# Exponents formed on ScalarE in five narrowings, and another opening of batch 0, in a Fourier-mixing and gated-convolution kernel

## The chip, the cores and the metric

The kernel runs on one core of one Trainium2 chip. The metric is device time in microseconds: the median of several executions. A profile is one further execution, recorded by the hardware profiler; its times count from the start of its span.

## The reference

```python
def _attn_ref(x):                       # x: (8, 3136, 256) float32
    X = np.fft.fft(x, axis=1)
    X = np.fft.fft(X, axis=2)
    return X.real.astype(np.float32)

def _moe_ref(x, w_in, conv_w, w_out):   # w_in 256x1024, conv_w 3x1024, w_out 1024x256
    h = np.maximum(x @ w_in, 0.0)
    # conv_out[s] = sum over k of conv_w[k] * h[s + k - 1], zeros outside
    gate = 1.0 / (1.0 + np.exp(-conv_out))
    return (h * gate @ w_out).astype(np.float32)

def reference(x, moe_w_in, moe_conv_w, moe_w_out):
    return _moe_ref(_attn_ref(x), moe_w_in, moe_conv_w, moe_w_out)
```

The three weights arrive as float64 (the division by a numpy float64 root makes them so); `x` and the output are float32.

## The kernel before

**The mathematics as the kernel lays it out.** The real part of a two-dimensional Fourier transform is computed by products with cosine and sine tables. Symmetry halves both axes: rows of `x` are folded with their mirrored rows (`fold_ops`, lines 143 to 200, on VectorE, with small parts on GpSimd), and the feature axis likewise. The sequence transform gives two spectra of a batch, `pt` and `qt` (`PQ[b]`), with 1569 columns. The feature transform is not done on its own: it is multiplied into `w_in` once, into the tile `G`, by `blocks(i)` for four blocks of `w_in`.

A hidden row `h` is then relu(a + c) in front and relu(a - c) behind, where a comes from `pt` and c from `qt`. Feature D/2 of the spectrum doesn't fit into the 128 rows of a product. It is kept as one row, `er[0]` for batch 0, spread to 128 partitions (`eb`), and added by ScalarE: `seed` writes `eb` times a weight column (`ge`, made by `column(i)`) into the PSUM tile `pa` before the product accumulates onto it.

**Turns.** The main loop runs over steps (batch, chunk, filter): 8 batches, 4 chunks of columns, 8 filters of 128 hidden features; 32 steps a batch. The order on each engine is the order of emission (`manual_schedule`): turn t emits, in this order, the sigmoid of step t-2, the products and copies of step t+1, side work "act", `combine` of step t, side work "dve", `seed` of step t+2, the first tap of step t, the other two taps of step t-1, the gate of step t-2, side work "load", the output products of step t-3, and side work "pe". Side work is put into turns by `at(turn, place, fn)`.

- `products` (L653 before): `pb` from `qt` and `pa` from `pt`, on TensorE. In a "triple" step (batch 0, the first 20 steps) a third product adds c to `pa` too, so that ScalarE can write the front half of `h` by a Relu straight from `pa` (`copies`, L672). In the other steps ScalarE copies `pb` twice (L675) and VectorE forms both halves (`combine`, L686).
- The taps: the first on ScalarE (L692), the other two on VectorE (L698, two instructions of 770 elements). The gate: half on GpSimd (L718), half on VectorE (L719).
- `mm2`: six or seven products with `w_out` into `po` (L733), and in the last filter the copies out and the stores on SP.

PSUM: `psa` has two tiles (`pa`), `psb` one (`pb`), `psd` one (`pd`), `pso` four (`po`, shared with the opening's `spare()`).

**Narrowing float64 weights.** `narrow` (L508) makes a float32 from the two 32-bit words of a float64 in seven VectorE operations: exponent bits out (L515), rebias (L516), shift back (L517), sign in (L518), mantissa top with hidden bit (L520), add the low word (L521), multiply (L522). It runs in four pieces for `w_in` (128x512 each), once for the convolution weights, and in four pieces for `w_out`, in turns 2, 3, 5 and 7; the last piece of `w_in` is in turn 0.

**The opening of batch 0.** TensorE is kept busy by products whose result is not used (`keep_on`), then the units of the sequence transform run: four odd ones, then by hand the units 2, 4, 3, 7, 8, where 2, 3, 7 and 8 are the even ones and 4 is the feature unit. Each unit has matmuls, a ScalarE copy and a `fin`: VectorE operations (L291 and L294 for even units), or four GpSimd operations for the feature unit (L353, L354), which complete `er[0]`. `row()` brings `er[0]`'s first content by a DMA; `flip()` (L366) negates every fourth column on ScalarE; `store()` writes the row to DRAM (`ed`); `spread` (L463) reads it back to all partitions, one transfer a chunk, into the four buffers of `eb`.

In batch 0's first four steps (`FIRST`) no `eb` is used: a product with one contraction row, `left[0:1]` by `er[0]`, adds feature D/2 to `pa` on TensorE; its weights are made in `blocks(0)` and `blocks(1)`. The `pa` tiles of steps 4 and 5 are first written over all 512 columns by a product (`start_all`, L640)[...]. The feature rows of batches 1 to 7 come from class `Feature`, whose tile takes the place of `er[0]` in its pool of one buffer.

Of the kernel before, what the change touches and what calls it, by code (L numbers as in the profile page):

```python
# [26 lines left out]

TRIPLE = 20  # L30
FIRST = 4
RC = 56
NQ = 8
CUTS = (0, 384, 768, 1152)
# [4 lines left out]
def kernel(  # L39
# [23 lines left out]
    NF = F // P  # L63
# [6 lines left out]
    const = ctx.enter_context(tc.tile_pool(name="const", bufs=1))  # L70
# [4 lines left out]
    ebp = ctx.enter_context(tc.tile_pool(name="ebp", bufs=4))  # L75
# [14 lines left out]
    stt = nc.vector.scalar_tensor_tensor  # L90
    act = nc.scalar.activation

    def mm(o, l, r, start, stop):
        nc.tensor.matmul(o, l, r, start=start, stop=stop, skip_group_check=True)  # L94

    def spare():

        return pso.tile([P, 2, D], F32, name="po", tag="po").rearrange("p a d -> p (a d)")
# [4 lines left out]
    xh, wt, ea = {}, {}, {}  # L103
# [3 lines left out]
    sg = const.tile([P, 2, 2], F32, name="sg")  # L107
# [97 lines left out]
    PQ, eb, er = {}, {}, {}  # L205
# [257 lines left out]
    def spread(b, cs):  # L463

        for c in cs:
            ch = chunks[c]
            eb[b, c] = ebp.tile([P, HN], F32, name="eb", tag="eb")[:, 0:ch.k1 - ch.k0]
            nc.sync.dma_start(out=eb[b, c], in_=ed[b:b + 1, ch.k0:ch.k1].to_broadcast([P, ch.k1 - ch.k0]))
# [36 lines left out]

    def narrow(dst, raw):  # L508

        ts = nc.vector.tensor_scalar  # L510
        lsl, lsr = ALU.logical_shift_left, ALU.logical_shift_right
        lo, hi = raw[:, :, :, 0], raw[:, :, :, 1]
        lof, d = lo.bitcast(F32), dst.bitcast(I32)

        ts(out=d, in0=hi, scalar1=20, scalar2=0x7FF, op0=lsr, op1=ALU.bitwise_and)  # L515
        ts(out=d, in0=d, scalar1=-896, scalar2=0, op0=ALU.add, op1=ALU.max)  # L516
        ts(out=d, in0=d, scalar1=23, scalar2=None, op0=lsl)  # L517
        stt(out=d, in0=hi, scalar=-0x80000000, in1=d, op0=ALU.bitwise_and, op1=ALU.bitwise_or)  # L518

        ts(out=hi, in0=hi, scalar1=0xFFFFF, scalar2=0x100000, op0=ALU.bitwise_and, op1=ALU.bitwise_or)  # L520
        stt(out=lof, in0=lo.bitcast(U32), scalar=2.0 ** -32, in1=hi, op0=ALU.mult, op1=ALU.add)  # L521
        stt(out=dst, in0=lof, scalar=2.0 ** -20, in1=dst, op0=ALU.mult, op1=ALU.mult)  # L522

    class Weight:

# [7 lines left out]
        def load(self, eng):  # L533
            if self.raw is None:
                eng.dma_start(out=self.dst, in_=self.src)
            else:
                eng.dma_start(out=self.raw.rearrange("p c n e -> p c (n e)"), in_=self.src)

        def narrow(self, c0, c1):
            if self.raw is not None:  # L540
                narrow(self.dst[:, c0:c1], self.raw[:, c0:c1])

    ident = gp.tile([3 * NF, 3 * NF], F32, name="ident", tag="g")
    make_identity(nc, ident)
    cw24 = gp.tile([3 * NF, 1, P], F32, name="cw24", tag="g")
# [10 lines left out]
    dm = gp.tile([P, 2, 2, P], F32, name="dm", tag="g")  # L556
    N4 = F // 4
# [28 lines left out]

    def blocks(i):


        w = w4[i]  # L590
        for g in range(2):
            p = spare()
            for t in range(2):
                mm(p[:, 0:N4], dm[:, t, g, :], w[:, t], t == 0, t == 1)
            nc.scalar.copy(out=G[:, g, i * N4:(i + 1) * N4], in_=p[:, 0:N4])
        if 2 * i < FIRST:
            p = spare()
            for t in range(2):
                mm(p[0:1, N4:2 * N4], dm[:, t, 1, P - 1:P], w[:, t], t == 0, t == 1)
            nc.scalar.copy(out=left[0:1, 2 * i:2 * i + 2].rearrange("p f i -> p (f i)"), in_=p[0:1, N4:2 * N4])  # L600
        if i > 1:
            column(i)

    def column(i):
        w, p = w4[i], spare()
        for m in range(NF // 4):
            for t in range(2):
                mm(p[:, m:m + 1], w[:, t, m * P:(m + 1) * P], dm[:, t, 1, P - 1:P], t == 0, t == 1)
        nc.scalar.copy(out=ge[:, i * NF // 4:(i + 1) * NF // 4], in_=p[:, 0:NF // 4])
# [7 lines left out]
    rows = out.rearrange("b s d -> (b s) d")  # L617
    hs, gs, pa, pb, po, nb = {}, {}, {}, {}, {}, {}

    def start_all(p, l, r):  # L620

        mm(p, l, r, True, True)

    def cut(s):
        b, c, f = s
        ch = chunks[c]
        return ch, ch.k1 - ch.k0, slice(f * P, (f + 1) * P)

    def first(s):

        return s[0:2] == (0, 0) and s[2] < FIRST

    def seed(s):

        b, c, f = s
        ch, n, fs = cut(s)
        pa[s] = psa.tile([P, 512], F32, name="pa", tag="pa")
        if not first(s):
            if s in ((0, 0, FIRST), (0, 0, FIRST + 1)):
                start_all(pa[s].rearrange("p (t n) -> p t n", t=2), dm[:, 0, 0], w4[0])  # L640
            act(pa[s][:, 0:n], eb[b, c], AF.Copy, scale=ge[:, f:f + 1])  # L641

    def triple(s):

        return s[0] == 0 and s[1] * NF + s[2] < TRIPLE

    def row_of(s):
        hs[s] = hp.tile([P, HW], F32, name="h", tag="h")
# [4 lines left out]
    def products(s):  # L653
        b, c, f = s
        ch, n, fs = cut(s)
        pb[s] = psb.tile([P, 512], F32, name="pb", tag="pb")
        mm(pb[s][:, 0:n], G[0:P - 1, 1, fs], PQ[b][1][0:P - 1, ch.k0:ch.k1], True, True)
        mm(pa[s][:, 0:n], G[:, 0, fs], PQ[b][0][:, ch.k0:ch.k1], first(s), not triple(s))
        if first(s):
            mm(pa[s][:, 0:n], left[0:1, f, :], er[b][:, ch.k0:ch.k1], False, False)  # L660
        if triple(s):
            mm(pa[s][:, 0:n], G[0:P - 1, 1, fs], PQ[b][1][0:P - 1, ch.k0:ch.k1], False, True)

    def copies(s):

        ch, n, fs = cut(s)
        p = pb.pop(s)
        nb[s] = nbp.tile([P, 2, HN], F32, name="nb", tag="nb")
        if triple(s):
            act(nb[s][:, 1, ch.cols], p[:, ch.cols], AF.Copy, scale=-2.0)  # L670
            row_of(s)
            act(hs[s][:, ch.front], pa[s][:, ch.fcols], AF.Relu)  # L672
# [34 lines left out]
    def sigmoid(s):  # L707

        v, p, r = shares(s)
        for c in (slice(p.start, r.stop), v):  # L710
            act(gs[s][:, c], gs[s][:, c], AF.Sigmoid)  # L711
# [33 lines left out]
    taps()  # L745
    idle = psb.tile([P, 512], F32, name="pb", tag="pb")

    def keep_on(n):

        for _ in range(n):  # L750
            mm(idle[:, 0:2 * P], wt[0][1][0:NP, 1, 0], wt[0][1][0:NP, 0, 0:2], True, True)

    begin, us, row, flip, store = units(0)
    begin()
# [4 lines left out]

    odds = [us[j] for j in (0, 1, 5, 6)]  # L760
    w_in[0].narrow(0, 2)
    keep_on(16)
    mirror_tables(0)
    mend_row(1, half)
    mirror_tables(2)
# [10 lines left out]
                    w_out.load(nc.sync)  # L776
    mend_row(0, half)
    w_in[1].narrow(0, 2)
    for i, u in enumerate(us[j] for j in (2, 4, 3, 7, 8)):
        u.matmuls(0, 1)  # L780
        u.copy()
        u.fin()
    flip()
    store()
    spread(0, range(len(chunks)))
    for f in load_ops(1, 0, nc.sync):
        f()
    blocks(0)
# [5 lines left out]
    def at(cycle, where, fn):  # L794
        side.setdefault((cycle, where), []).append(fn)

    for i in (1, 2, 3):
        at(i - 1, "pe", lambda i=i: blocks(i))
    at(0, "dve", lambda: w_in[3].narrow(0, 2))
    for i in (0, 1):  # L800
        at(i, "pe", lambda i=i: column(i))
    for cycle, c in ((2, 0), (3, 2), (5, 4), (7, 6)):
        at(cycle, "dve", lambda c=c: w_out.narrow(c, c + 2))
    for j, fn in enumerate(load_ops(1, 1, nc.sync)):
        at(NF + 1 + j // 3, "load", fn)

# [57 lines left out]
    seed(steps[1])  # L864
    products(steps[0])
    copies(steps[0])
    for t in range(n + LAG):
        def run(where):
            for fn in side.get((t, where), []):
                fn()  # L870
        if 0 <= t - 2 < n:
            sigmoid(steps[t - 2])
        if t + 1 < n:
            products(steps[t + 1])
            copies(steps[t + 1])
# [12 lines left out]
        run("load")  # L888
        if t >= LAG:
            mm2(steps[t - LAG])  # L890
        run("pe")
# [66 lines left out]
```

## Time and profile before

| what | value |
|---|---|
| median of 10 runs | 1218.14 us (1217.46 to 1219.17) |
| profiled execution, its own time | 1219.29 us |
| its span | 1217.5 us |
| TensorE busy | 1185.7 us, 97% of the span |
| VectorE busy | 1124.8 us, 92% |
| ScalarE busy | 877.8 us, 72% |
| GpSimd busy | 373.4 us, 31% |
| chain that ended last, by engine | PE 69%, DVE 21%, issue 4%, ACT 2%, DMA 1% |

The profiled execution took 1.79 us more than its span, and 1.15 us more than the median. PE is TensorE, PEld its weight loads, DVE VectorE, ACT ScalarE, POOL GpSimd, SP the engine that issues most DMAs. A busy share is a mean over stages with different limits, so the stages are to be read one by one. Most of the work is recorded under one line for TensorE (L94, the helper `mm`), so its rows are told apart by tiles.

### The profile page before, as it was taken

What the parts mean: (1) busy time and instruction counts of PE and PEld (TensorE: products, weight loads), DVE (VectorE), ACT (ScalarE), POOL (GpSimd) and SP (SyncE); (2) the same over time, 40 slices, a digit from 0 to 9 for tenths busy, and PEclk for the clock granted to TensorE, in tenths of its full rate; (3) what the DMA queues carried; (4) which work ended last, traced back from release to release, by engine and by line L of the source; (5) the groups of instructions that cost most, each with busy time, mean ns of one, the idle gap of its engine ahead of it and who ended that gap; (6) DMA issues with size and microseconds to landing.
All of it is one profiled execution on the core that took longest, in us unless ns stands there. A gap on an engine that the chain in (4) does not pass through costs nothing.

```text
span 1217.5 us, 15448 instructions
## 1 busy us (share of the span) xinstructions
PE 1185.7 (97%) x4876; PEld 906.8 (74%) x4876; DVE 1124.8 (92%) x1696; ACT 877.8 (72%) x1832; POOL 373.4 (31%) x474
## 2 busy tenths in 40 slices
PE   5999999999999999999999999999999999999998
PEld 4676777677777777777777777777777777777776
DVE  7799999999999999998999999999998988899996
ACT  2466656676777777777777777777777777788884
POOL 5224524343334232424224242332222222222222
PEclk9999999999999999999999999999999999999999
DMA  9622243211121110302122020210001000110000
GB/s 218 198 8 80 80 49 100 68 53 41 40 87 50 60 46 1 107 26 73 34 73 61 5 80 27 88 46 26 27 1 53 31 26 27 46 33 27 26 27 31
DMA packets 70213, 66.30 MB, mean 54 GB/s; under 512 B 28123, under 2 KB 57827, under 8 KB 70131
## 3 DMA queue, kind: packets, MB, share of 16 engines
q1 hardware_dynamic: 64493, 52.18, 15.2%
q0 software_dynamic: 5120, 12.85, 3.5%
q8 instruction: 39, 0.64, 0.2%
q14 instruction: 43, 0.35, 0.1%
q10 hardware_dynamic: 518, 0.28, 0.1%
HBM read 39.53 MB, written 25.74 MB: 54 GB/s over the span
## 4 chain that ended last, share of the span: by engine, by line
PE 69%; DVE 21%; issue 4%; ACT 2%; DMA 1%; DVEq 0%; SPq 0%; ACTq 0%
PE po L94 43%; PE pb L94 10%; PE pa L94 10%; DVE g L698 7%; PE pd L94 6%; DVE h L686 3%; DVE g L719 3%; DVE xh L158 2%; ACT nb L675 1%; DVE xh L169 1%; DVE w L186 1%; DVE w L187 1%; DMA xh<-in_x_dram 0%; DVE xh L173 0%; DVE pt L291 0%
## 5 line engine op out<-in xcount | busy, mean ns | idle before, releaser
L94 PE MATMUL po<-wout,g 128*128 128x256 f32 x3072 | 709.0, 380 | 10.9 <-DVE g L719 10.3
L94 PEld LDWEIGHTS po<-wout,g 128*128 128x128 f32 x3072 | 578.7, 190 | 164.0 <-DVE g L719 43.6
L698 DVE SCALAR_TENSOR_TENSOR g<-h,cw,g 128x770 f32<-128x770 f32 (+1 forms) x512 | 548.7, 1072 | 9.3 <-ACT g L692 0.2
L718 POOL TENSOR_TENSOR g<-g,h 128x385 f32<-128x385 f32 (+1 forms) x256 | 234.1, 915 | 767.0 <-ACT g L711 496.1
L711 ACT ACTIVATE g<-g 128x385 f32<-128x385 f32 (+2 forms) x512 | 244.1, 526 | 191.4 <-DVE g L698 188.9
L675 ACT ACTIVATE nb<-pb 128x386 f32<-128x386 f32 (+2 forms) x472 | 208.0, 493 | 85.6 <-PE pb L94 84.6
L686 DVE CUSTOM_DVE_ANT_0 h<-pa,nb 128x386 f32<-128x386 f32 (+2 forms) x492 | 255.5, 559 | 3.7 <-ACT h L672 3.7
L692 ACT ACTIVATE g<-h,cw 128x770 f32<-128x770 f32 (+1 forms) x256 | 243.2, 950 | 0.2 <-DVE h L686 0.2
L94 PE MATMUL pb<-qt,G 127*128 127x387 f32 (+2 forms) x512 | 212.6, 496 | 0.0
L94 PE MATMUL pa<-pt,G 128*128 128x387 f32 (+2 forms) x512 | 211.8, 494 | 0.0
L641 ACT ACTIVATE pa<-eb,ge 128x387 f32<-128x387 f32 (+2 forms) x252 | 151.4, 601 | 1.3 <-PE pa L94 0.7
L94 PEld LDWEIGHTS pa<-pt,G 128*128 128x128 f32 x512 | 96.8, 189 | 73.6 <-issue 18.2
L719 DVE TENSOR_TENSOR g<-g,h 128x385 f32<-128x385 f32 (+1 forms) x256 | 146.1, 571 | 0.9 <-ACT g L711 0.9
L94 PE MATMUL pd<-tab,w 98*128 98x196 f32 (+3 forms) x448 | 126.7, 374 | 0.0
L133 POOL DMA_INDIRECT xh<-in_x_dram,idx x64 | 105.5, 1649 | 13.3 <-issue 9.2
L94 PEld LDWEIGHTS pb<-qt,G 127*128 127x128 f32 x512 | 94.0, 190 | 17.9 <-issue 1.4
L94 PEld LDWEIGHTS pd<-tab,w 98*128 98x128 f32 (+1 forms) x448 | 84.7, 191 | 12.3
L738 ACT COPY os<-po 128x256 f32<-128x256 f32 x196 | 57.4, 393 | 8.2 <-PE po L94 4.6
L158 DVE TENSOR_TENSOR xh<-xh 98x1020 f32<-98x1020 f32 (+1 forms) x32 | 40.7, 1277 | 3.4 <-DMA xh<-in_x_dram,idx 3.4
L169 DVE TENSOR_TENSOR xh<-xh 98x1024 f32<-98x1024 f32 (+1 forms) x32 | 41.3, 1290 | 0.1
L188 POOL COPY w<-xh 98x4 f32<-98x4 f32 (+1 forms) x32 | 20.2, 632 | 28.0 <-DVE xh L169 14.8
L291 DVE TENSOR_TENSOR qt<-as,pd 128x197 f32<-128x197 f32 (+1 forms) x14 | 7.2, 514 | 20.3 <-ACT as L287 20.3
(114 smaller groups left out, 394.0 us busy)
## 6 DMA issues: line engine op xcount, KB each, us to landing
out_dram<-os SPq DMA_DIRECT2D x192, 128.0 KB
xh<-in_x_dram SPq DMA_DIRECT2D x16, 784.0 KB
eb<-ed SPq DMA_DIRECT2D x16, 193.5 KB
tab<-dft_seq_dram SPq DMA_DIRECT2D x4, 589.5 KB
raw<-in_moe_w_in_dram SPq DMA_DIRECT2D x4, 512.0 KB
raw<-in_moe_w_out_dram SPq DMA_DIRECT2D x1, 2048.0 KB
eb<-ed SPq DMA_DIRECT2D x8, 209.0 KB
eb<-ed SPq DMA_DIRECT2D x8, 193.0 KB
```

Source lines behind the costliest of these rows:

```text
L94: nc.tensor.matmul(o, l, r, start=start, stop=stop, skip_group_check=True)
L133: nc.gpsimd.indirect_dma_start(out=xh[b, h][0:NP, 7 - m].rearrange("p q d -> p (q d)"), out_offset=None, in_=bass.AP(tensor=x.tensor, offs ...
L158: vt(a[:, :, :, 1:D], a[:, :, :, 1:D], r[:, :, :, D - 1:0:-1], op=ALU.add)
L641: act(pa[s][:, 0:n], eb[b, c], AF.Copy, scale=ge[:, f:f + 1])
L675: act(nb[s][:, i, cols], p[:, cols], AF.Copy, scale=-1.0 if i else 1.0)
L686: nc.vector._custom_dve(TENSOR_ADD_SAT, out=to, in0=a[:, cols], in1=c[:, i, cols], s0=BIG, s1=0.0)
L692: act(gs[s], hs[s][:, 0:n], AF.Copy, scale=cw[:, 0, s[2]:s[2] + 1])
L698: stt(out=g, in0=h[:, k:k + n], scalar=cw[:, k, f:f + 1], in1=g, op0=ALU.mult, op1=ALU.add)
L711: act(gs[s][:, c], gs[s][:, c], AF.Sigmoid)
L718: gt(g[:, p], g[:, p], h[:, p], op=ALU.mult)
L719: vt(g[:, v], g[:, v], h[:, v], op=ALU.mult)
L738: nc.scalar.copy(out=osb[:, j % 2], in_=pt[:, j % 2])
```

## The change

Seven edits, in three groups.

1. `narrow` can be given a scratch tile (`room`, the upper half of `left`). Then rebias and shift are one ScalarE activation, a Relu with scale 2^23 and a bias tile `low` of -896 x 2^23; the sign comes in after the mantissa, and the masked mantissa goes to `room`. It is split: `power` (one VectorE operation and the Relu) is emitted in a new place "first", after the sigmoid; `product` (four VectorE operations) stays in "dve". This form is used in five narrowings: the last of `w_in`, and all four of `w_out`. The other three of `w_in` keep seven operations.
2. Triple steps begin at step 3 instead of 0. Steps 0 to 2 copy `pb` twice and form both halves on VectorE.
3. `FIRST` and what belongs to it goes: the one-row products in steps 0 to 3, their weights in `blocks`, and `start_all`. All steps are seeded. The feature unit becomes the first of the five units, followed by `flip`, `store` and the spread of chunks 1 to 3; chunk 0's `eb` comes from a product of a row of ones with `er[0]` on TensorE and a ScalarE copy. `column(0)` and `column(1)` move ahead. The keep-on products become 8 of 512 columns instead of 16 of 256, two of them into the `pa` tiles. There are two more small memsets at the start.

```diff
-TRIPLE = 20
-FIRST = 4
+TRIPLE = 3, 20
...
+    low = const.tile([P, 1], F32, name="low")
+    nc.gpsimd.memset(low, -896.0 * 2 ** 23)
+    def narrow(dst, raw, room=None):
...
+        sg = hi
+        if room is not None:
+            c, n = hi.shape[1:]
+            sg = room[:, 0:c * n].rearrange("p (c n) -> p c n", c=c)
+        def power():
+            ts(out=d, in0=hi, scalar1=20, scalar2=0x7FF, op0=lsr, op1=ALU.bitwise_and)
+            if room is not None:
+                act(d, d, AF.Relu, scale=2.0 ** 23, bias=low[0:d.shape[0]])
+            else:
+                ts(out=d, in0=d, scalar1=-896, scalar2=0, op0=ALU.add, op1=ALU.max)
+                ts(out=d, in0=d, scalar1=23, scalar2=None, op0=lsl)
+        def sign():
+            stt(out=d, in0=hi, scalar=-0x80000000, in1=d, op0=ALU.bitwise_and, op1=ALU.bitwise_or)
+        def product():
+            if room is None:
+                sign()
+            ts(out=sg, in0=hi, scalar1=0xFFFFF, scalar2=0x100000, op0=ALU.bitwise_and, op1=ALU.bitwise_or)
+            stt(out=lof, in0=lo.bitcast(U32), scalar=2.0 ** -32, in1=sg, op0=ALU.mult, op1=ALU.add)
+            if room is not None:
+                sign()
+            stt(out=dst, in0=lof, scalar=2.0 ** -20, in1=dst, op0=ALU.mult, op1=ALU.mult)
+        return power, product
...
+    one = const.tile([1, P], F32, name="one")
+    nc.gpsimd.memset(one, 1.0)
...
-        if 2 * i < FIRST:
-            p = spare()
-            for t in range(2):
-                mm(p[0:1, N4:2 * N4], dm[:, t, 1, P - 1:P], w[:, t], t == 0, t == 1)
-            nc.scalar.copy(out=left[0:1, 2 * i:2 * i + 2].rearrange("p f i -> p (f i)"), in_=p[0:1, N4:2 * N4])
...
-        if not first(s):
-            if s in ((0, 0, FIRST), (0, 0, FIRST + 1)):
-                start_all(pa[s].rearrange("p (t n) -> p t n", t=2), dm[:, 0, 0], w4[0])
-            act(pa[s][:, 0:n], eb[b, c], AF.Copy, scale=ge[:, f:f + 1])
+        act(pa[s][:, 0:n], eb[b, c], AF.Copy, scale=ge[:, f:f + 1])
...
-        return s[0] == 0 and s[1] * NF + s[2] < TRIPLE
+        return s[0] == 0 and TRIPLE[0] <= s[1] * NF + s[2] < TRIPLE[1]
...
-        mm(pa[s][:, 0:n], G[:, 0, fs], PQ[b][0][:, ch.k0:ch.k1], first(s), not triple(s))
-        if first(s):
-            mm(pa[s][:, 0:n], left[0:1, f, :], er[b][:, ch.k0:ch.k1], False, False)
+        mm(pa[s][:, 0:n], G[:, 0, fs], PQ[b][0][:, ch.k0:ch.k1], False, not triple(s))
...
-    keep_on(16)
+    keep_on([idle] * 6)
+    keep_on([psa.tile([P, 512], F32, name="pa", tag="pa") for _ in range(2)])
...
-    for i, u in enumerate(us[j] for j in (2, 4, 3, 7, 8)):
+    for i, u in enumerate(us[j] for j in (4, 2, 3, 7, 8)):
         u.matmuls(0, 1)
         u.copy()
         u.fin()
-    flip()
-    store()
-    spread(0, range(len(chunks)))
+        if i == 0:
+            flip()
+            store()
+            spread(0, range(1, len(chunks)))
+    n = chunks[0].k1
+    p = psd.tile([P, 512], F32, name="pd", tag="pd")
+    mm(p[:, 0:n], one, er[0][:, 0:n], True, True)
+    eb[0, 0] = ebp.tile([P, HN], F32, name="eb", tag="eb")[:, 0:n]
+    nc.scalar.copy(out=eb[0, 0], in_=p[:, 0:n])
+    column(0)
...
-    at(0, "dve", lambda: w_in[3].narrow(0, 2))
-    for i in (0, 1):
-        at(i, "pe", lambda i=i: column(i))
+    room = left[:, NF // 2:].rearrange("p f i -> p (f i)").bitcast(I32)
+    def shared(cycle, w, c):
+        for where, fn in zip(("first", "dve"), w.parts(c, c + 2, room)):
+            at(cycle, where, fn)
+    shared(0, w_in[3], 0)
     for cycle, c in ((2, 0), (3, 2), (5, 4), (7, 6)):
-        at(cycle, "dve", lambda c=c: w_out.narrow(c, c + 2))
+        shared(cycle, w_out, c)
...
     copies(steps[0])
+    column(1)
...
             sigmoid(steps[t - 2])
+        run("first")
```

More of the change, by code (lines that the diff above doesn't have):

```diff
@@ L503 @@
     left = const.tile([P, NF, P], F32, name="left")
-    def narrow(dst, raw):
+    low = const.tile([P, 1], F32, name="low")
+    nc.gpsimd.memset(low, -896.0 * 2 ** 23)
+    def narrow(dst, raw, room=None):
         ts = nc.vector.tensor_scalar
@@ L513, in narrow @@
         lof, d = lo.bitcast(F32), dst.bitcast(I32)
[L515 to L522, printed above, removed]
+        sg = hi
[20 more added lines that the diff above has]
+        return power, product
     class Weight:
@@ L537, in load, with parts @@
                 eng.dma_start(out=self.raw.rearrange("p c n e -> p c (n e)"), in_=self.src)
+        def parts(self, c0, c1, room=None):
+            if self.raw is None:
+                return []
+            return narrow(self.dst[:, c0:c1], self.raw[:, c0:c1], room)
         def narrow(self, c0, c1):
-            if self.raw is not None:
-                narrow(self.dst[:, c0:c1], self.raw[:, c0:c1])
+            for f in self.parts(c0, c1):
+                f()
+    one = const.tile([1, P], F32, name="one")
+    nc.gpsimd.memset(one, 1.0)
     ident = gp.tile([3 * NF, 3 * NF], F32, name="ident", tag="g")
@@ L618 @@
     hs, gs, pa, pb, po, nb = {}, {}, {}, {}, {}, {}
-    def start_all(p, l, r):
-        mm(p, l, r, True, True)
     def cut(s):
@@ L627, in cut @@
         return ch, ch.k1 - ch.k0, slice(f * P, (f + 1) * P)
-    def first(s):
-        return s[0:2] == (0, 0) and s[2] < FIRST
     def seed(s):
@@ L746, with keep_on @@
     idle = psb.tile([P, 512], F32, name="pb", tag="pb")
-    def keep_on(n):
-        for _ in range(n):
-            mm(idle[:, 0:2 * P], wt[0][1][0:NP, 1, 0], wt[0][1][0:NP, 0, 0:2], True, True)
+    def keep_on(banks):
+        for p in banks:
+            mm(p.rearrange("p (s q d) -> p s q d", s=2, q=2), wt[0][1][0:NP, 1, 0], wt[0][1][0:NP, 0:2, 0:2],
+               True, True)
     begin, us, row, flip, store = units(0)
```

## The prediction

> **What bounds the kernel now.** I read the page first, then busy time by stretch, then the waits, then the chain and timeline of the first 95 us, the only part whose code changes.
>
> ```profile
> PE 1185.7 (97%) x4876; PEld 906.8 (74%) x4876; DVE 1124.8 (92%) x1696; ACT 877.8 (72%) x1832; POOL 373.4 (31%) x474
> ```
>
> Two engines are near full, so the question is which sets the pace where. Busy time by stretch (us; PE, PEld, DVE, ACT, POOL, then clock, DMA share, GB/s):
>
> ```profile
> 58.00:95.00 37.00, 35.55 (x148) 25.58 (x147) 35.65 (x54) 23.86 (x48) 7.82 (x18) 1.00 0.20 16
> 130.00:170.00 40.00, 38.98 (x162) 29.17 (x161) 39.11 (x53) 25.52 (x54) 18.99 (x19) 1.00 0.41 68
> 290.00:330.00 40.00, 40.00 (x166) 30.71 (x166) 38.04 (x58) 28.82 (x61) 15.14 (x15) 1.00 0.16 53
> ```
>
> From 58 us, VectorE is busy over 96% (35.65 of 37) and TensorE waits for it now and then; from 290 us TensorE is full. So a microsecond won by both before turn 8 moves all that follows: the turns after it are unchanged, and their loads are issued turn by turn. Inside the opening, VectorE's longest waits (total us, times, longest):
>
> ```profile
> DVE h L686 <- ACT h L672: 3.7, 2, 2.8
> ```
>
> The chain around it (start, us):
>
> ```profile
> 55.35 2.35 PE pa L94 x6
> 57.74 0.04 issue
> 57.79 0.50 ACT h L672
> 58.29 0.02 issue
> 58.31 0.56 DVE h L686
> ...
> 59.24 0.44 DVE wout L516
> 59.68 0.02 issue
> 59.70 0.44 DVE wout L517
> ```
>
> Until 58.3 us TensorE leads (six passes, three products into `pa`: spectrum, one-row, third), ScalarE's Relu follows, VectorE idles 2.82 us. From there VectorE leads, with the seven operations of a narrowing. ScalarE's timeline, for what is queued in front of its sigmoid:
>
> ```profile
> 58.17 0.94 ACT L692 ACTIVATE g<-h,cw 128x770 f32<-128x770 f32 x1
> 59.01 0.82 ACT L595 COPY G<-po 128x256 f32<-128x256 f32 x2
> 60.24 0.16 ACT L609 COPY ge<-po 128x2 f32<-128x2 f32 x1 [0.41 <-PE po L94]
> 61.13 0.16 ACT L609 COPY ge<-po 128x2 f32<-128x2 f32 x1 [0.73 <-PE po L94]
> 61.31 1.28 ACT L711 ACT_TABLE_LOAD   x1
> 62.61 0.94 ACT L711 ACTIVATE g<-g 128x385 f32<-128x385 f32 x2
> ```
>
> And two waits of SP's queue:
>
> ```profile
> SPq L468 <- ACT pa L641: 46.0, 7, 9.7
> ...
> SPq L369 <- DMA er<-qt: 1.0, 1, 1.0
> ```
>
> **What the Trainium skill says.** (1) "ScalarE: Activation LUTs", What ACT_TABLE_LOAD costs: a load about 1.28 us, and an ACTIVATE with a per-partition bias 0.28 us + 0.833 ns an element; the trace agrees (load 1.28; L692 with a per-partition scale, 770 elements, 0.93). For the new Relu, 512 elements, I estimate 0.28 + 0.43 = 0.71, back to back less. (2) "GPSIMD Engine Reference", Specifications: its SBUF interfaces are shared with VectorE, against operations with two SBUF inputs or in a two-port mode. The trace agrees: under a POOL gate L521 takes 1.24 instead of 0.69, L517 0.97 instead of 0.43: about 0.5 a turn, before and after alike. (3) "TensorE: Matmul & The Clock Gate", Why this matters for your kernels: few contraction rows save a single product no time. The trace agrees: one-row products start 0.84 apart (46.19 to 47.03), full ones of the same width 0.65.
>
> **The change, part by part** (times on before's clock).
>
> *Opening, feature unit first.* Its 8 products (0.88) move from 36.80 to 35.20; ScalarE's copies (1.31 for four) begin at 36.1 and the third, which POOL needs, ends at 37.15. The row `er` lands later: SP finished issuing at 36.32 and waited 1.0 for it, so 37.35. POOL's four operations took 3.07 (38.80 to 41.87): 37.4 to 40.5. The flip (0.93) then ends at 41.45. **The added wait:** the flip stands on ScalarE ahead of all four copies `as<-po`, for which VectorE's eight fins wait: the first copy ends at 41.77, the first fin starts at 41.82 instead of 40.75. Cost +1.07; eight fins (2.84) end at 44.66 instead of 43.59.
>
> *Spread by a product.* TensorE's rows are the same up to 41.75. Then the one-row product (0.84), column 0 (0.89 by 53.54 to 54.43), block 0 (1.72, four at 0.43): 45.2. ScalarE's two copies to `G` end at 45.75, so the first `pb` starts at 45.85 instead of 44.70: +1.15 on TensorE. On SP one `eb` transfer goes; the other three and the x load move up, and nothing waits for them (SP's x load went at 47.13, used from turn 9). The three gathers behind `er` (5.19 of SP) no longer wait for the one-row products (63.38), and move beside the x load; first use is turn 14. But `eb` buffers now rotate one off: chunk 2 of a batch waits for the buffer of the last batch's chunk 3, free at turn 32b-3. SP waits there already (46.0 us in 7, above); the wait moves two transfers up, ahead of an x load used some 7 turns (32 us) later. Zero, with that cover.
>
> *Warm-up.* 8 products of 512 columns for 16 of 256: the same columns; zero, give or take 0.3. The two 512-column resets (L640) are replaced by it.
>
> *Third and one-row products, turns 0 to 2.* TensorE loses 3 x 0.65, 4 x 0.84, the two resets 2 x 0.65 and in blocks 0 and 1 2 x 0.95, gains 0.84: 7.7 less. It is worth only the waits that it ends: the 0.91 and 2.82 of VectorE. ScalarE gains four seeds (0.58 each), inside its idle time. VectorE gains three front halves (0.47 each).
>
> *VectorE to the first tap.* Narrowing 2 (4.07 by 43.59 to 47.66, unchanged): 44.66 to 48.73. Head of narrowing 3 (0.46) 49.19, both halves of turn 0 (0.94) 50.13, its four others (0.46 + 0.73 + 0.73 + 0.69 by L520, L521, L518, L522) 52.74, both halves of turn 1 53.68, taps of turn 0 (2.07) 55.75. Before: 55.49. So far 0.26 behind.
>
> *Turn 2, where it is decided.* VectorE: head 56.2, halves 57.15, two operations 58.34; the sign operation needs the Relu. ScalarE from 49.2: Relu 49.9, `nb` of turn 1 (0.86) 50.75, seed 51.25, first tap 52.1, `G` (0.82) 52.95. TensorE: turn 2's products 53.0 to 54.3, block 2 56.0, column 2 56.95. ScalarE: `ge` 57.15, table load 57.3 to 58.6, sigmoid 59.55, Relu 60.2. So VectorE **stalls 1.9** to 60.25, finishes the narrowing (1.42) 61.68 and the taps (2.07, POOL's gate now falls into the stall) 63.75, where before they ended at 65.17: 1.42 ahead.
>
> *Turns 3, 5, 7.* Each narrowing loses two operations of 0.46: 3 x 0.92 = 2.76. No stall: in turn 3 the sigmoid ends at 64.7, the Relu at 65.4, and VectorE reaches the sign at 63.75 + 0.47 + 0.46 + 0.47 + 0.46 + 0.73 = 66.34. What is late next: TensorE's output product of turn 0 starts at 64.3 (gate) instead of 70.32, and its pace is 4.54 (70.32, 74.86, 79.40), so that of turn 5 could start at 87.0; VectorE lets it at 94.78 - 1.42 - 2.76 = 90.6. VectorE still decides, and TensorE is ahead by as much.
>
> *Sum.* 1.42 + 2.76 = 4.18; two more memsets ahead of POOL's first gathers (0.03 each by 0.93, 0.96, 0.99) take 0.06: **-4.1 us**. Span 1217.5 to 1213.4, own time of the profiled execution 1219.29 to 1215.2; that execution stands 1.15 above the median, so the median goes 1218.14 to **1214.0**.
>
> *Not shown by this trace.* Relu on int32: at least 0.55 (a `pa` copy of 386 elements with a scale takes 0.58), at most 0.9; the stall moves by as much, -0.15 to +0.2. First-mask into another tile: -0.1 to +0.3 a narrowing, I take 0. POOL against VectorE: one more or fewer overlap in each of four turns, -1 to +1. With these the likeliest case runs from 1212.5 to 1215.6.
>
> **Rivals.**
> *No stall in turn 2.* If ScalarE comes 1.9 earlier (its queue was read off one timeline), 6.0 are won: 1212.1. Against it: table load, sigmoid and Relu are 2.9 in a row behind `ge`.
> *The gain is given back.* A stage after turn 8 starts at something that didn't move, SP's loads or a buffer: 0 to 2.4 won, about 1217. For it: SP's 46 us of waits. Against: VectorE waited for DMA only before 11 us, 7.3 us in three waits.
> *Slower: ScalarE's queue becomes the bound.* Place: the sign operation in turns 2, 3, 5, 7 behind sigmoid and Relu. Each 0.92 of wait eats a narrowing's saving; with 1.4 more in each of the three turns the whole gain is gone, at 2.8 it is 1222.3. For it: the 1.07 at the flip and 1.9 in turn 2 are such waits. Against: from the end of the taps to the sign, ScalarE has sigmoid and Relu in front of it (1.65), VectorE gate, head, half and two operations (2.59): 0.9 to spare, if ScalarE's queue is empty by then.
> *The change doesn't do what it says*: excluded for the counts, since the instruction streams show two operations fewer on VectorE in each of five narrowings.
>
> **How the numbers follow.** Forecast 0.60, no stall 0.11, given back 0.15, slower 0.14. A measurement tells about 0.2%, 2.4 us. Faster 0.60 + 0.11 = 0.71; same 0.15; slower 0.14. Range: down to 1211.5 for the better rival with its bounds, up to 1217.0 for half of the third; the rest and the slower case are left out.
>
> **What would show it.** Right: no DVE wait for L672 in turns 0 to 2; flip ending near 41.5; a VectorE gap of 1 to 3 us at about 58 to 60 before the sign operation; first output product near 64.3, the sixth near 90.6; VectorE's and TensorE's later rows earlier by one constant. Wrong: VectorE gaps before the sign in turns 3, 5, 7; an offset that shrinks after 95 us; a new DMA wait.

## Result: 1218.36 to 1211.67 us, and the profile after

On one chip, with the runs of the two kernels in turn, the kernel before took 1218.36 us (median of 28 runs) and the changed one 1211.67 (8 runs, 1211.08 to 1213.26): a ratio of 0.9948, 95% interval 0.9939 to 0.9957. That is 6.7 us less, where 4.1 were forecast. The profiled execution took 1212.72 us with a span of 1211.0, so span and own time fell by 6.5 and 6.6 as well.

The page's busy times (us, share of the span, instructions) after the change:

```profile
PE 1177.0 (97%) x4836; PEld 899.3 (74%) x4836; DVE 1121.5 (93%) x1689; ACT 881.6 (73%) x1840; POOL 373.4 (31%) x476
```

VectorE lost 3.3 us of work, half of the gain, and TensorE 8.7, more than the gain; the shares hardly moved. Where the 6.5 us come from can't be read from totals, only from the waits and the timeline. Two of the stretches of busy time by engine, as before (PE, PEld, DVE, ACT, POOL, then clock, DMA share, GB/s):

```profile
58.00:95.00 37.00, 34.59 (x140) 25.26 (x139) 35.68 (x50) 26.85 (x54) 11.00 (x20) 1.00 0.15 28
...
290.00:330.00 40.00, 40.00 (x164) 30.24 (x164) 37.76 (x57) 28.74 (x61) 14.19 (x14) 1.00 0.12 38
```

They look as before: from 58 us VectorE is near full (35.68 of 37), from 290 us TensorE is. The limits have not changed hands; the same pattern starts earlier. Of the waits (us in total, times, longest), VectorE's 3.7 us for ScalarE's Relu of `h` (two waits) is gone, and one new wait stands in the list; SP's wait for the `eb` buffer is what it was (46.0 before):

```profile
DVE wout L532 <- ACT wout L526: 2.0, 1, 2.0
...
SPq L467 <- ACT pa L653: 45.9, 7, 9.7
```

L532 is the sign operation of a narrowing, L526 the new Relu on ScalarE. ScalarE's timeline shows what the Relu of turn 2 is queued behind (start, duration, both in us; a last bracket is idle time and what ended it):

```profile
55.78 0.16 ACT L632 COPY ge<-po 128x2 f32<-128x2 f32 x1 [0.41 <-PE po L93]
55.96 1.28 ACT L721 ACT_TABLE_LOAD   x1
57.26 0.94 ACT L721 ACTIVATE g<-g 128x385 f32<-128x385 f32 x2
58.10 0.71 ACT L526 ACTIVATE wout<-wout,low 128x512 int32<-128x512 int32 x1
```

The table load and the two halves of the sigmoid (2.14 us from 55.96 to 58.10) stand ahead of a Relu of 0.71. Before, this load began at 61.31.

**Where the gain lies in time.** The best mark is VectorE's gate, which stands once in each turn. Its starts in the two timelines (L719 before, L729 after):

| gate in turn | before | after | step to the last one, before | after | difference |
|---|---|---|---|---|---|
| 2 | 65.17 | 62.16 | | | -3.01 |
| 3 | 72.53 | 68.06 | 7.36 | 5.90 | -1.46 |
| 4 | 75.98 | 71.48 | 3.45 | 3.42 | -0.03 |
| 5 | 83.35 | 77.33 | 7.37 | 5.85 | -1.52 |
| 6 | 86.83 | 81.75 | 3.48 | 4.42 | +0.94 |
| 7 | 94.17 | 87.61 | 7.34 | 5.86 | -1.48 |

The gate of turn 7, after the last narrowing, is 6.56 earlier, and the span is 6.5 shorter. All of the gain is made by then, and the rest of the program is shifted as a whole. Two parts of these differences are not work saved in the turns: 0.51 of the 3.01 is there already when the transform's first products start at 25.69 instead of 26.20, and the 0.94 lost in turn 6 is missing from the profiles of most kernels below. Both are taken up again in the part on the prediction.

### The profile page after: what moved, and what is told of

The parts are those of the page before. It is cut to its first block, busy times and chain, and to the rows that moved or that the text cites. A ratio compares the mean times of both kernels' runs of the same rounds, so it can differ in the third digit from the quotient of the medians.

```text
span 1211.0 us, 15374 instructions
## 1 busy us (share of the span) xinstructions
PE 1177.0 (97%) x4836; PEld 899.3 (74%) x4836; DVE 1121.5 (93%) x1689; ACT 881.6 (73%) x1840; POOL 373.4 (31%) x476
## 4 chain that ended last, share of the span: by engine, by line
PE 69%; DVE 22%; issue 4%; ACT 3%; POOL 1%; DMA 1%; DVEq 0%; SPq 0%; POOLq 0%; ACTq 0%
PE po L93 43%; PE pb L93 11%; PE pa L93 10%; DVE g L708 7%; PE pd L93 6%; DVE h L696 3%; DVE g L729 3%; DVE xh L157 2%; ACT nb L685 1%; DVE xh L168 1%; DVE w L185 1%; POOL xh L132 1%; DVE w L186 1%; DMA xh<-in_x_dram 0%; DVE pt L290 0%
## 5 line engine op out<-in xcount | busy, mean ns | idle before, releaser
L685 ACT ACTIVATE nb<-pb 128x386 f32<-128x386 f32 (+2 forms) x478 | 210.6, 493 | 85.0 <-PE pb L93 84.0
L729 DVE TENSOR_TENSOR g<-g,h 128x385 f32<-128x385 f32 (+1 forms) x256 | 146.1, 571 | 0.9 <-ACT g L721 0.9
```

The source lines that it names most:

```text
L729: vt(g[:, v], g[:, v], h[:, v], op=ALU.mult)
```

## Experiments

The theory to test (A): the two groups of edits work only together. The new opening ends VectorE's waits for the long triple steps, the shared narrowings shorten turns 3, 5 and 7, and what is won up to turn 7 moves the rest of the program one to one. The rivals: one group brings nearly all of it; or the wait in turn 2 is harmless because something else is late. Each kernel is compared with the kernel before on the same chip. "Gate 2" and "gate 7" are the starts of VectorE's gate in turns 2 and 7 in the profile (65.17 and 94.17 before, 62.16 and 87.61 after). In some profiles TensorE's granted clock falls to half in the opening (last section); such a profile is set beside that of e10, which is the changed kernel with the same fall.

**e1: the shared narrowings alone**, on the opening of before.

```diff
-    at(0, "dve", lambda: w_in[3].narrow(0, 2))
+    shared(0, w_in[3], 0)
     for cycle, c in ((2, 0), (3, 2), (5, 4), (7, 6)):
-        at(cycle, "dve", lambda c=c: w_out.narrow(c, c + 2))
+        shared(cycle, w_out, c)
...
             sigmoid(steps[t - 2])
+        run("first")
```

> The five shared narrowings alone, on the opening of before. Theory A (the two groups need each other): in turns 3, 5 and 7 VectorE gains 1.5 us each as in the changed kernel, but in turn 2 ScalarE reaches the table load at 61.3 as before, so the Relu ends near 64.2 and the sign operation waits for it; the taps of turn 1 end near 67.6 instead of 65.2. Sum -4.5 + 2.4 = about -2 us, 1216.3. Rival B (savings add up, each narrowing is worth 0.92 to 1.5 wherever it stands): 5 x 0.92 to 5 x 1.5, -4.6 to -7.5 us, 1210.9 to 1213.8.

Measured: 1216.35 us against 1218.19, ratio 0.9984 (0.9977 to 0.9990); gate 7 at 92.12, span 2.1 less. VectorE's timeline has both waits in turn 2, for the triple step's Relu of `h` and then for the narrowing's Relu:

```profile
58.38 0.56 DVE L713 CUSTOM_DVE_ANT_0 h<-pa,nb 128x385 f32<-128x385 f32 x1 [3.52 <-ACT h L699]
64.26 0.69 DVE L533 SCALAR_TENSOR_TENSOR wout<-raw,wout 128x512 int32<-128x512 int32 x1 [4.26 <-ACT wout L527]
```

VectorE works less and waits more: the wait for ScalarE is 4.26 instead of the 2.03 of the whole change, because the `ge` copies, table load and sigmoid ahead of the Relu still run late behind the old opening. 1.8 of the 6.7 us come from this group alone, as theory A expected.

**e2: the opening and the triple steps alone**, all narrowings with seven operations on VectorE.

```diff
     def shared(cycle, w, c):
-        for where, fn in zip(("first", "dve"), w.parts(c, c + 2, room)):
-            at(cycle, where, fn)
+        at(cycle, "dve", lambda: w.narrow(c, c + 2))
```

> The opening and the triple steps of the changed kernel, but all narrowings on VectorE with seven operations. Theory A: the 2.0 us wait for the Relu in turn 2 goes, the narrowings of turns 0 and 2 get 1.2 longer each, so the taps of turn 1 end near 62.5 instead of 62.2; turns 3, 5 and 7 get 1.5 longer each: about +4.9 us on the changed kernel, 1216.5, that is -1.8 on before. Rival B (adding up: the whole minus the narrowings): the opening alone is worth 6.7 - 4.6 = 2.1 at most, near the same here, so this run tells the theories apart only together with the narrowings alone: A wants the two parts to sum to about -4, B to -6.7.

Measured: 1216.75 us against 1218.19, ratio 0.9988 (0.9979 to 0.9996). Between 36 and 95 us its profile has no VectorE wait at all. Its gate 7 is 3.95 earlier and its span 3.9 less, but that execution's opening was early: the first odd product of the sequence transform began at 24.58 us, against 26.20 before and 25.69 after; the 13 runs reach from 1215.2 to 1219.2, so I read this kernel by its median. The two groups give 1.84 + 1.44 = 3.3 us one by one and 6.7 together. That is what theory A says, and neither group alone carries the result. Which edit inside the second group does how much is tested by e7 and e8 for two of them only.

**e3: the sigmoid's table loaded in the idle start**, so that turn 2 has no load.

```diff
+    act(low[0:1], low[0:1], AF.Sigmoid)
+    nc.gpsimd.memset(low, -896.0 * 2 ** 23)
     w_cv.narrow(0, 1)
```

> The changed kernel with one tiny sigmoid on ScalarE at the very start, so that the only table load is at the start. Theory A (in turn 2 VectorE's sign operation waits for table load, sigmoid and Relu, and the opening decides for all that follows): the wait shrinks from 2.03 to about 0.75, and the whole shifts by 1.28: 1210.4. Rival C (the opening's gain is given back, or another wait steps in at once): within 0.4 us of the changed kernel.

Measured: 1211.12 us, ratio to before 0.9941 (0.9928 to 0.9955). The wait before the sign operation is 1.29 instead of 2.03, and 1.4 less than in e10's profile, which has the same fall of the clock (2.70): the 1.28 of the load. Against e10's, gate 2 is 1.47 earlier (61.78 and 63.25), so what the wait loses is handed on; gate 7 is 2.44 earlier (86.31 and 88.75), of which 0.93 is turn 6. In the medians little of it shows: 1210.4 was expected, and 1211.12 is only 0.5 below the changed kernel, inside the spread of these five runs. That the wait in turn 2 sets the end rests on e4 and e11.

**e4 and e11: the Relu ahead of the sigmoid in turn 2** (one kernel, run on two chips).

```diff
+        if t == 2:
+            run("first")
         if 0 <= t - 2 < n:
             sigmoid(steps[t - 2])
-        run("first")
+        if t != 2:
+            run("first")
```

> The changed kernel with the Relu of turn 2 emitted ahead of the table load and the sigmoid on ScalarE. Theory A: the Relu ends near 56.7, when VectorE reaches the sign operation, so no wait; the sigmoid ends 0.65 later (58.8), before VectorE needs it (60.2): -2.0 us, 1209.7. Rival C: within 0.4 us of the changed kernel, since the sigmoid that comes later or TensorE decides next.

Measured in e4: 1210.46 us against 1218.19 before, ratio 0.9939 (0.9926 to 0.9953); gate 7 at 85.22, 2.39 earlier than after, and span 8.8 less than before. There is no VectorE wait left between 36 and 95 us. ScalarE's Relu now comes right behind the `ge` copy, and VectorE's taps follow its narrowing without a gap:

```profile
55.71 0.72 ACT L526 ACTIVATE wout<-wout,low 128x512 int32<-128x512 int32 x1
56.45 1.28 ACT L721 ACT_TABLE_LOAD   x1
```

```profile
57.91 2.56 DVE L708 SCALAR_TENSOR_TENSOR g<-h,cw,g 128x770 f32<-128x770 f32 x2
```

The taps took 2.56 instead of 2.08: GpSimd's gate (58.41 to 59.66) now lies beside them, where in the changed kernel it lay in VectorE's wait. So the wait of 2.03 brought the first gate forward by 1.76 (60.40 instead of 62.16). Of the rest of the 2.39, turn 6 gave 0.94, since it took its old time here, and turn 3 took 0.29 back, since GpSimd's gate there met a longer operation (6.19 between the gates instead of 5.90). The kernel was run again beside the changed one on another chip:

> The changed kernel with the Relu of turn 2 ahead of the table load, again, for a comparison on one chip. Theory (the 2.0 us wait in turn 2 is gone, less about 0.5 for GpSimd's gate that now meets VectorE's taps): -1.2 to -2.0 against the changed kernel. Rival (no lasting gain): within 0.4.

> The changed kernel once more, beside the next two on the same chip: 1211.7 us, and the gate of turn 7 near 87.6 us of its span, give or take 1 us by how the first transfers land.

Measured: the changed kernel 1211.60 (1211.16 to 1213.96), with the Relu first 1209.84 (1208.84 to 1210.26), the kernel before 1218.21. The ratios to before are 0.9947 (0.9934 to 0.9961) and 0.9930 (0.9916 to 0.9943). The five runs of each do not overlap: 1.8 us less, inside the 1.2 to 2.0 expected. How much of it is the wait and how much turn 6, the medians don't separate: both profiles of the changed kernel have the long turn 6, those of e4 and e11 don't. This is the version that beats both kernels. (Gate 7 of e10, at 88.75, missed its forecast of 87.6 give or take 1: its clock fell.)

**e5: a flip that does wait for GpSimd**, by two copies of one element each, which read what GpSimd writes, ahead of it.

```diff
+            nc.scalar.copy(out=left[0:1, 0, 0:1], in_=er[b][:, M - 2:M - 1])
+            nc.scalar.copy(out=left[0:1, 0, 1:2], in_=er[b][:, Q4 + 2:Q4 + 3])
             act(er[b][:, 3:NK:4], er[b][:, 3:NK:4], AF.Copy, scale=-1.0)
```

> The changed kernel with two copies of one element of er[0] on ScalarE ahead of the flip, so that the flip really waits for GpSimd's last operation, as the prediction had it. The prediction's step: the four copies as<-po and the eight fins start 1.0 us later, about +1.0 us. Revised theory (the flip touches only columns 3 mod 4, which GpSimd doesn't write; and VectorE is busy with narrowing 1 until 40.8 anyway, while GpSimd ends near 39.6): flip to about 40.7, first fin near 41.2 instead of 40.8: +0.2 to +0.5 us.

Measured: 1212.31 us (1211.50 to 1215.08) against 1218.46, ratio 0.9960 (0.9945 to 0.9974). ScalarE now waits 3.13 us for GpSimd ahead of the flip, and yet VectorE's first fin waits only 0.25:

```profile
38.88 0.19 ACT L365 COPY left<-er 1x1 f32<-1x1 f32 x1 [3.13 <-POOL er L353]
...
39.07 0.92 ACT L367 ACTIVATE er<-er 1x392 f32<-1x392 f32 x1
```

```profile
40.37 0.51 DVE L290 TENSOR_TENSOR qt<-as,po 128x197 f32<-128x197 f32 x1 [0.25 <-ACT as L286]
```

Until 40.1 VectorE is busy with a narrowing. Even where the wait exists, it is hidden but for 0.25 us. The medians, 1212.31 and 1211.67, are too near each other to show more.

**e6: the head of each shared narrowing at "dve"**, behind `combine`, instead of at "first".

```diff
-        for where, fn in zip(("first", "dve"), w.parts(c, c + 2, room)):
+        for where, fn in zip(("dve", "dve"), w.parts(c, c + 2, room)):
```

> The changed kernel with the first half of each shared narrowing (one VectorE operation and the Relu) emitted where the second half is, not at the head of the turn. Theory: the Relu then stands behind the copies of the next step on ScalarE, which wait for TensorE; the sign operation waits 1 us more in turn 2 and 0.5 to 1 in turns 5 and 7, nothing in turn 3: +1 to +2.5 us. Rival (VectorE's two operations between head and sign, 1.1 us, cover the Relu anywhere): 0 to +0.3.

Measured: 1215.09 us (1213.60 to 1216.88) against 1218.46, ratio 0.9973 (0.9962 to 0.9984). The sign operation waits 0.49 in turn 0, 3.14 in turn 2, nothing in turn 3, 0.28 in turn 5 and 0.23 in turn 7. Its profile is set beside e10's: gate 7 at 90.68 and 88.75, 1.93 later. The waits before the sign operation and in `combine` are 1.96 more in sum. The head (L524), now behind `combine`, meets GpSimd's gate in turns 3 and 5 and takes 1.01 and 0.94 instead of 0.42, where in the changed kernel a later operation met it (0.67 and 0.62 instead of 0.43); against that, turn 6 has none of the 0.94 us which e10 has. So by the medians half of the gain (3.4 of 6.7 are left) hangs on where the head is put, more than the 2.5 expected at most. But in turns 3 to 7 ScalarE's queue costs 0.28 a turn at most, even with the later head.

**e7: triple steps from step 0**, all else as in the change.

```diff
-TRIPLE = 3, 20
+TRIPLE = 0, 20
```

> The changed kernel with the third product in steps 0 to 2 again. Theory (until turn 2 TensorE leads, through the copies of G, into ScalarE's queue with the table load): two of the three third products come ahead of block 2, 1.3 us later there, so the Relu of turn 2 and all after it are 1.3 later: +1.3 us. Rival (VectorE's three front halves, 0.47 each, are what counts): -1.4 us.

Measured: 1213.19 us (1212.62 to 1215.58) against 1218.46, ratio 0.9959 (0.9945 to 0.9974). VectorE waits 1.40 and 0.98 for ScalarE's Relu of `h` in turns 0 and 2, 0.76 for a first tap in turn 1, and 3.37 before the sign operation in turn 2 (e10, with the same fall of the clock, waits 0.34 in `combine` and 2.70 before the sign operation, and nowhere else). The three front halves more that VectorE does in the change (steps 0 to 2) cost less than those waits; the triple steps' edit is worth some 1.4 us of the 6.7 (5.3 are left without it), as the theory said.

**e8: chunk 0's `eb` from DRAM too**, without the product with ones.

```diff
-            spread(0, range(1, len(chunks)))
+            spread(0, range(len(chunks)))
-    n = chunks[0].k1
-    p = psd.tile([P, 512], F32, name="pd", tag="pd")
-    mm(p[:, 0:n], one, er[0][:, 0:n], True, True)
...
-    nc.scalar.copy(out=eb[0, 0], in_=p[:, 0:n])
```

> The changed kernel with chunk 0 of the feature row spread by DMA like the other three, in place of the product with ones and its copy. Theory: the store to DRAM has landed at 43.4, the spread needs about 2 us more (an estimate from the store's own 3.4), so the first seed starts near 46 instead of 44.9, and TensorE saves 0.84; 0 to +1 us. Rival (transfer shares the DMA engines with w_out and the gathers and takes 5 us or more): +2 us or more.

Measured: 1216.20 us (20 runs) against 1218.46, ratio 0.9981 (0.9974 to 0.9988): 4.4 of the 6.7 us are lost, where the theory gave 1 at most. ScalarE's first two seeds wait for the transfer:

```profile
47.54 1.09 ACT L653 ACTIVATE pa<-eb,ge 128x386 f32<-128x386 f32 x2 [2.29 <-DMA eb<-ed]
```

The row leaves for DRAM at 40.18 (SP's store), the reads are issued from 43.08, and the seeds start at 47.54. VectorE then waits 1.67, 0.68 and 1.34 in `combine` and 3.35 before the sign operation. This need not all be the transfer: TensorE, which waited 1.97 for the first seed, had its clock at 0.50 from 48.6 to 55.5, and all 20 runs have a mean clock of 0.994 to 0.996. How the 4.4 divides is not shown. Seeding from step 0 works without the product with ones, and still beats the kernel before by 2.3; with it, it pays in full.

**e9: seven shared narrowings**: e4, and the second and third pieces of `w_in` shared with ScalarE as well.

```diff
-    w_in[1].narrow(0, 2)
...
+            for f in w_in[1].parts(0, 2, room):
+                f()
...
+    power, product_ = w_in[2].parts(0, 2, room)
+    power()
...
-    w_in[2].narrow(0, 2)
+    product_()
```

> The same, with narrowings 1 and 2 of w_in shared with ScalarE too. Theory: narrowing 1 and 2 get 1.2 to 1.5 shorter each on VectorE; the fins then wait for the last copy as<-po (41.4), and the first combine for its nb (46.9 instead of 48.15), where TensorE and ScalarE lead: about -1.2 more, near 1209. Rival (the opening is led by TensorE's and ScalarE's chain already): within 0.4 of the run before.

Measured: 1209.89 us (1208.88 to 1212.24) against 1218.21, ratio 0.9934 (0.9920 to 0.9947), beside 1209.84 for e11 on the same chip: nothing more, where the theory gave 1.2 and the rival none. In its profile, what VectorE saves ahead of turn 0 it waits for:

```profile
48.52 1.02 DVE L696 CUSTOM_DVE_ANT_0 h<-pa,nb 128x385 f32<-128x385 f32 x2 [2.07 <-PE pa L93]
```

There TensorE and its copies lead ahead of turn 0, not VectorE. But this profile has the fall of the clock, which put TensorE's first `pb` at 46.77 (45.08 in the change's); without it the wait would be shorter, by how much no profile shows. What holds is the medians: sharing two more narrowings brought nothing that can be measured.

## Why the prediction was right, and where its sum was short

The direction, the mechanism and the constant shift held; the forecast of 1214.0 was 2.3 us too high. In the profile the gate of turn 2 came 1.6 earlier than forecast, turns 3, 5 and 7 saved 1.7 more, and turn 6 took 0.9 back. Luck had a part in it: 1211.67 lies below the likeliest case (1212.5 to 1215.6) and only 0.2 above the lower end of the range, which was drawn for the rival without a stall.

**"The added wait" at the flip, +1.07: wrong, there was none; and the warm-up, "zero", was not zero.** The step put the flip behind GpSimd's four operations, at 41.45. The timelines of ScalarE and GpSimd, after the change:

```profile
36.55 0.94 ACT L365 ACTIVATE er<-er 1x392 f32<-1x392 f32 x1
```

```profile
36.55 0.65 POOL L352 TENSOR_TENSOR er<-as 1x197 f32<-1x197 f32 x1 [9.81 <-ACT as L344]
...
38.84 0.78 POOL L353 TENSOR_TENSOR er<-as 1x196 f32<-1x196 f32 x1
```

The flip ran at 36.55, beside GpSimd. It negates columns 3, 7, 11 and so on, and GpSimd's operations write only even columns, so there is no dependence; `er[0]` in both did not mean the same elements. And e5 shows that the wait, made real, would have been hidden behind VectorE's narrowing but for 0.25. The first fin started at 40.81 (forecast 41.82; before 40.75). That 1.01 has two halves. The opening stood 0.51 ahead from the first products of the sequence transform on, before and after:

```profile
26.20 8.10 PE L94 MATMUL po<-tab,w 98*128 98x196 f32 x32
```

```profile
25.69 8.10 PE L93 MATMUL po<-tab,w 98*128 98x196 f32 x32
```

They start when the keep-on products end. The two profiles with the old opening have 26.20 and 26.26, the eleven with the new one 24.58 to 25.95; so the new warm-up seems worth 0.25 to 1.7 us, where the prediction gave it zero, give or take 0.3. No run changed it alone. The other half is the missing wait of 1.07, less 0.57: the narrowing ahead of the fins took 4.89 us instead of 4.32, with GpSimd's four operations beside it (L532 took 0.90 there and 0.69 undisturbed, L538 0.72 and 0.43). TensorE's first `pb` came at 45.08 (forecast 45.85; before 44.70).

**VectorE to the first taps.** Forecast: taps of turn 0 end at 55.75, 0.26 behind the kernel before; measured 54.48, 1.0 ahead. Of the 1.27, 1.01 stands at the first fin, 0.35 is a shorter turn 0 (the reordered narrowing, below), and 0.11 went to a narrowing of 4.18 instead of 4.07.

**"Turn 2, where it is decided": right.** The stall forecast at 1.9 was 2.03, behind what the step named (the table load and the sigmoid), and e4 and e11 show that it counts. The Relu priced at 0.71 took 0.71. All of it came 1.4 earlier than forecast, since its queue did, so the gate of turn 2 was at 62.16 instead of 63.75: 3.0 ahead, not 1.42. The rival without a stall named 1212.1, nearer to the result than the forecast, and is wrong all the same: the stall was there.

**"Turns 3, 5, 7 ... two operations of 0.46": the mechanism was right, the size was not.** Each turn saved 1.46 to 1.52 instead of 0.92, 4.46 in the three instead of 2.76. VectorE in turn 3, after and then before (lines of the narrowing that differ):

```profile
62.63 0.42 DVE L524 TENSOR_SCALAR wout<-raw 128x512 int32<-128x512 int32 x1
62.97 0.55 DVE L696 CUSTOM_DVE_ANT_0 h<-pa,nb 128x385 f32<-128x385 f32 x1
63.44 0.67 DVE L538 TENSOR_SCALAR left<-raw 128x512 int32<-128x512 int32 x1
64.14 0.69 DVE L539 SCALAR_TENSOR_TENSOR raw<-raw,left 128x512 f32<-128x512 uint32 x1
64.76 0.68 DVE L532 SCALAR_TENSOR_TENSOR wout<-raw,wout 128x512 int32<-128x512 int32 x1
```

```profile
66.11 0.41 DVE L515 TENSOR_SCALAR wout<-raw 128x512 int32<-128x512 int32 x1
66.55 0.43 DVE L516 TENSOR_SCALAR wout<-wout 128x512 int32<-128x512 int32 x1
...
67.47 0.69 DVE L518 SCALAR_TENSOR_TENSOR wout<-raw,wout 128x512 int32<-128x512 int32 x1
68.20 0.43 DVE L520 TENSOR_SCALAR raw<-raw 128x512 int32<-128x512 int32 x1
68.66 1.24 DVE L521 SCALAR_TENSOR_TENSOR raw<-raw 128x512 f32<-128x512 uint32 x1
```

Read starts, not durations. Before, each operation of the narrowing needs the one ahead of it: it reads what that one wrote or, in L520, overwrites what L518 reads. L515 to L516 is 0.44 apart. After, the head L524 is followed by a front half that doesn't need its result, and the next start is 0.34 later; L539 to L532, now independent, are 0.62 apart, where L518 to L520 were 0.73 (67.47 to 68.20). Together that is some 0.23 a turn. The third part, about 0.3, is GpSimd: its gate met L521 before (1.24 instead of 0.69), and meets L538 now (0.67 instead of 0.43), a shorter operation. In turns 5 and 7 it met L517 and L515 before (0.97 and 0.92) and L538 now (0.62 and 0.63), 0.3 again. The step that fell short is thus "two operations of 0.46" as the whole of a turn's saving: what it left out, the order and the place of GpSimd's gate, was worth more than half as much (0.54 against 0.92). The part of the gate hangs on the timing: in e4 it met L539 in turn 3 (1.24), and 0.29 was lost again.

**Contention of GpSimd with VectorE: in its bound, and against the change.** Turn 6 has no narrowing and took 0.94 more. VectorE's taps and GpSimd's work beside them (small memsets for the next batch's feature row, then a gate), after:

```profile
78.34 3.49 DVE L708 SCALAR_TENSOR_TENSOR g<-h,cw,g 128x770 f32<-128x770 f32 x2
```

```profile
78.19 0.90 POOL L410 MEMSET ft<- 1x393 f32 x4
79.10 0.85 POOL L728 TENSOR_TENSOR g<-g,h 128x385 f32<-128x385 f32 x1
```

And before:

```profile
84.36 2.55 DVE L698 SCALAR_TENSOR_TENSOR g<-h,cw,g 128x770 f32<-128x770 f32 x2
```

```profile
84.21 0.90 POOL L411 MEMSET ft<- 1x393 f32 x4
85.11 0.98 POOL L718 TENSOR_TENSOR g<-g,h 128x385 f32<-128x385 f32 x1
```

The pair of taps took 2.07 undisturbed and 2.56 beside a gate, but 3.49 here; the longer one of the two took 2.43, where it took 1.51 before. Yet the memsets and the gate stand where they stood before, measured from the taps: 0.15 ahead, and 0.76 and 0.75 behind. The profiles of e5 and e10 have the 3.49 too, those of e1 to e4, e6 to e9 and e11 don't. What decides it is not shown. "GPSIMD Engine Reference", Specifications, in the Trainium skill says that the two engines share their way to SBUF; the 2.56 against 2.07 agrees, and the page gives no size.

**What is late next, and the constant offset: right.** TensorE's output products of turns 0 and 5:

```profile
62.77 2.86 PE L93 MATMUL po<-wout,g 128*128 128x256 f32 x12 [0.40 <-DVE g L729]
...
88.23 2.86 PE L93 MATMUL po<-wout,g 128*128 128x256 f32 x12 [0.92 <-DVE g L729]
```

Forecast were 64.3 and 90.6, with VectorE deciding; they came at 62.77 and 88.23 and waited for VectorE's gate. The slower rival, that ScalarE's queue delays the sign operation in turns 3, 5 and 7, did not come about: in the changed kernel there is no such wait after turn 2. "The gain is given back" did not either: in the profile of every kernel here the span differs from that of before by what gate 7 differs by, within 0.2 us. Two edits costed at nothing (`eb` buffers one off, SP's order) show no wait of their own; SP's 45.9 us are those of before.

## What to carry to other kernels

When two operations are removed from a chain of dependent ones, look at the order that is left: neighbours that don't need each other were worth 0.23 of the 1.46 us of a turn here. Before charging a wait to an operation that shares a tile with another engine's work, compare the elements, and then ask what else its followers wait for. When work is handed to another engine, ask what it is queued behind there: moving one Relu ahead of the table load and the sigmoid brought 1.8 us in the medians.

## What the runs showed of the chip

The changed kernel's times fall into two groups. Of its 15 executions on record, the nine with a mean granted TensorE clock of 1.000 took 1210.6 to 1211.7 us, the six with 0.998 or 0.999 took 1212.7 to 1214.0. The profile of e10 has a place for it; busy time in the stretch from 42 to 46 us, clock third from the end, in the profile of the change and in e10, the same kernel:

```profile
42.00:46.00 4.00, 3.54 (x19) 2.71 (x19) 3.86 (x11) 2.16 (x6) 2.58 (x7) 1.00 0.90 265
```

```profile
42.00:46.00 4.00, 4.00 (x16) 3.16 (x15) 3.86 (x11) 0.83 (x3) 3.13 (x7) 0.59 0.84 224
```

In e10 the clock was at 0.50 for 3.4 us from about 42.7, in the middle of an opening whose TensorE rows had the same starts within 0.04 us until then. The first `pb` came 1.73 later, the sign wait grew to 2.70, and gate 7 and the span came 1.1 to 1.2 later. The profiles of e3, e6, e7 and e9 have the same fall at the same place; those of before, after, e1, e2, e4, e5 and e11 don't.

Where VectorE leads, a fall cost nothing that can be seen. All 13 profiles have a wait of 1.92 to 1.96 us of TensorE for VectorE's gate between 199 and 211 us. In seven of them (e2, e3, e4, e5, e8, e9, e11) the clock falls to 0.50 for 3.4 us within 1.2 us of its end, in the other six it doesn't; and the span of the seven differs from that of before by what gate 7 differs by, as everywhere, within 0.2 us. So the mean clock alone says little: e11's fastest run (1208.84) has 0.997, its lowest, and the kernel before took 1217.8 to 1218.8 at 0.996, no more than at 1.000. The profile of the change itself, at 0.999, shows no fall, and why it took 1212.72 stays open.

"TensorE: Matmul & The Clock Gate", Part 1: The HAM clock gate, in the Trainium skill tells of a clock gate that halves the clock by the activity in a window of about 3.4 us, which runs freely of the kernel; the 0.50, the 3.4 us and the fall in some executions only agree. The page puts the half clock behind an idle window of about that length. Here 1.94 us of waiting were enough near 200 us, 1.97 in e8 (a fall from 48.6 to 55.5, twice 3.4), and at 42.7 no wait of TensorE stands ahead of it. That the thin stretch there (one-row weights, products of one column, 40.85 to 42.65) counts as idleness is a guess: of the ten profiles with the one-row product there, five have the fall and five don't; the three without it (before, e1, e8) don't, but they differ in more than that.
